# Retention plus GELU MLP on one core: w_out cast on two engines, batch 1's values cast by ScalarE, batch 2 turned by DMA

## The chip, the cores and the metric

The kernel runs on one core of a Trainium2 chip. The metric is the device time of one execution in microseconds (us); it was 302.02 us as the median of three executions (301.77 to 302.8). TensorE (PE) multiplies, VectorE (DVE), ScalarE (ACT) and GpSimd (POOL) do the elementwise work, and SyncE (SP) issues nearly all DMAs.

## The reference

For 8 batches, 8 heads, 576 positions and 64 values per head, a retention layer without a softmax feeds a two-layer MLP:

```
scores = (q @ k^T) / sqrt(64)                       # per batch and head, 576 x 576
ret    = scores * gamma[h]^(i-j) for i >= j, else 0  # gamma[h] = 1 - 2^(-5-h)
x      = (ret @ v), heads side by side               # 4608 tokens x 512
out    = gelu_tanh(x @ w_in) @ w_out                 # 512 -> 2048 -> 512
```

All inputs and the output are float32; the kernel computes in float16 with float32 sums.

## The kernel before, in words

**Blocks.** The MLP works on nine blocks of 512 tokens, t = 0 to 8. Block t < 8 is the first 512 positions of batch t; block 8 gathers the 64 last positions ("tails") of all batches. The retention of batch t + 1 is computed inside block t, in pieces that are hung between the MLP's steps. The 512 positions are four chunks of 128; a chunk's result needs its scores (`score`, `score2`, PE, tile `st`), the masked scores (`masks`, `masks2`, DVE, tile `ret`), and the running state of the chunks before it (`state`, `state2` on PE, tile `us`; `scan` on DVE, tiles `vs` and `ws`; `spread` on ACT, tile `tbd` or `tbt`). `past` and `av` / `av2` on PE add both into tile `xs`, and `put` on ACT writes `xT`, the MLP's input. `later` is `scan` and then `spread`.

**Order.** Every engine runs its instructions in the order in which the program emits them. A block is a list of steps, and `at(t, u, f)` hangs f behind step u of block t; negative u are the steps of block 0's first MLP half. Block 0: steps 0 to 15 are `down_mm` for output rows 0 to 255 (two matmuls each, one per f of w_out's 16 rows of tiles), step 16 is `store_pair`, steps 17 to 32 are `down_mm` for the other rows, step 33 is the second `store_pair`. Block 1: steps 0 to 15 are `up_half` (eight matmuls and one GELU each), then 14 steps `prod(m, u)` for the seven products of a Strassen-like scheme in the order 1, 6, 5, 7, 2, 3, 4, two halves u each. Blocks 2 to 8: steps 0 to 15 are `up`, then the same 14 steps. Products 1 and 2 sum into PSUM tile `opA`, 6, 7 and 4 into `opB`, 5 and 3 into `opC`; `after` (L574 adds on DVE, L590 and L604 copies on ACT) reads a sum out before the next product of that tile may write. `act_sums` (DVE, L542 to L545) makes the summed activations `s` that products 3, 5, 6 and 7 use, and `weight_sums` (DVE, L531) the summed weights `wt`.

**Loads.** All loads of q, k, v, w_in and w_out go through 16 buffers `ld` of 256 KB, in the order of the list `seq`: batch 0, 16 tiles of w_in, 16 of w_out, then batch by batch. A load may be issued once the buffer's former tile has been cast, and SP has at most 8 transfers in flight: each waits for the landing of the one eight before it. `pump` emits the loads that have a buffer, `q_ld["hold"]` stops it until `resume`. `cast` (line L251, L253, L256 or L264, called by `cc`) turns a loaded tile into float16 tiles `cq`, `ck`, `cv`, scaled by the decay for q and k. Batches 0 to 2 (`b < NPE`) are loaded so that two neighbouring positions come as one piece of 512 bytes; the others come in pieces of 256 bytes. `cq` has one buffer, `ck` and `cv` two.

**Turning.** Scores need q and k with the 64 values of a head on the partitions (tile `tt`). In batches 0 to 2 PE does that: `turn` is eight 128x128 transposes into a PSUM tile `tr` and one copy on ACT (L291), once for q and once for k in each half (group g) of a batch. From batch 3 on `turn_dma` has SP issue one DMA transpose for `ck` and one for `cq`, of 16 blocks of 128x128 each; in every second block a third one follows for two batches' tails (`ett`).

**Around the change.** The 16 casts of w_out (L630) are on POOL, behind four memsets (L710) and ahead of the mask constants `cm`, `tm` and all casts of batches 1 and 2. Batch 1's q is turned behind steps 19 and 32 of block 0 and k behind step 21 and step 0 of block 1; batch 2's turns hang behind steps 8, 9, 13 and 14 of block 1. Batch 3 is cast by POOL from step 16 of block 1 on, behind a one-element copy `gate` that waits for the last `act_sums`; its DMA transposes are emitted behind step 27.

Of the kernel before, what the change touches and what calls it, by code (L numbers as in the profile page):

```python
# [20 lines left out]
def kernel(  # L21
# [20 lines left out]
    W = NC * 512  # L42
    NB = W // 128
    NPE = 3
    LD = 16
    HOLD = 3
    TB = 512
    NI = TB // 128
    NTB = NT // TB
# [32 lines left out]
    def load_tails(b):  # L82
        a = att[PAIR + b] = {"raw": {}, "ret": {}}
        for key in "kqv":
            a["raw"][key, 0] = t = ldt()
            for n in range(2):
# [2 lines left out]
                    in_=SRC[key][b + n, :, M0:S, :].rearrange("h s d -> s h d"),  # L89
                )  # L90

    def load(b, key, c):
        src = SRC[key]
        t = lds()
        if b < NPE:
            g, y = c // 2, c % 2
            nc.sync.dma_start(  # L97
                out=t.rearrange("p (n x) -> p n x", n=4),
                in_=src[b, y::2, 256 * g : 256 * g + 256, :].rearrange("n (p j) d -> p n (j d)", j=2),
            )  # L100
        else:
            nc.sync.dma_start(
                out=t.rearrange("p (h d) -> p h d", d=D),
                in_=src[b, :, 128 * c : 128 * c + 128, :].rearrange("h s d -> s h d"),
            )
        att[b]["raw"][key, c] = t
# [11 lines left out]
        w_raw["o", f] = t  # L118

    def body(b):  # L120
        if b < NPE:
            return [("b", b, key, 2 * g + y) for g in range(2) for key in "qkv" for y in range(2)]
        return [("b", b, key, c) for c in range(NC) for key in "kqv"]

    seq = body(0) + [("i", g, ct) for g in range(4) for ct in range(4)]
    seq += [("o", f) for f in range(NF)]
    TP = {2: 0, 4: 2, 6: 4, 7: 6}
    for b in range(1, B):
        seq += body(b)
# [4 lines left out]
    def pump(freed=0):  # L134
        q_ld["free"] += freed
        while q_ld["next"] < len(seq) and not q_ld["hold"]:
            s = seq[q_ld["next"]]
            if s[0] != "t":
                if q_ld["free"] == 0:
                    return  # L140
                q_ld["free"] -= 1
            q_ld["next"] += 1
            {"b": load, "i": load_w_in, "o": load_w_out, "t": load_tails}[s[0]](*s[1:])
# [101 lines left out]
    def cast(b, key, c, eng):  # L245
        a = att[b]
        raw = a["raw"].pop((key, c))
        dst = a[key][:, 512 * c : 512 * c + 512]
        if key == "v":
            if eng is nc.scalar:  # L250
                eng.copy(out=dst, in_=raw)  # L251
            else:
                eng.tensor_copy(out=dst, in_=raw)  # L253
        elif b < NPE:
            y = c % 2
            eng.tensor_tensor(  # L256
                out=a[key][:, 1024 * (c // 2) : 1024 * (c // 2) + 1024].rearrange("p (n l d) -> p l n d", l=2, d=D)[:, y],
                in0=raw.rearrange("p (n d) -> p n d", d=D),
                in1=sp[key][:, :, y].unsqueeze(2).to_broadcast([128, 8, D]),
                op=ALU.mult,  # L260
            )
        else:
            s0 = {"q": 0, "k": 2}[key] + (b >= PAIR)
            eng.tensor_tensor(  # L264
                out=dst.rearrange("p (h d) -> p h d", d=D),
                in0=raw.rearrange("p (h d) -> p h d", d=D),
                in1=sc[:, s0].unsqueeze(2).to_broadcast([128, 8, D]),
                op=ALU.mult,
            )
# [21 lines left out]
            cp(out=o, in_=t)  # L291
            drop(full)

    def turn_dma(b, tails=None):
        a = att[b]
        for key in "kq":
            nc.sync.dma_start_transpose(out=a["t" + key], in_=a[key])
        if tails is not None:
            cast_tails(tails)

    def resume():
        q_ld["hold"] = False
        pump()

    def tq(b, c, p):
        return att[b]["tt"][:, 1, 8 * (c // 2) + 2 * p + c % 2 if b < NPE else 4 * c + p, :]

    TILES = [(h, hl) for h in range(2) for hl in range(2)]

# [109 lines left out]
    def spread(b, c, cp):  # L419
        w = att[b].pop(("w", c))  # L420
        for hl in range(2):
            r = slice(64 * hl, 64 * hl + 64)
            cp(out=(tbd[b % 2][r, c, :, r] if c < NC - 1 else tbt[b % NT4][r, :, r]), in_=w[r])  # L423
# [78 lines left out]
        return sb.tile([128, 2, DM], F32, tag="ost", name="ost", bufs=2)  # L502

    def down_mm(t, i, f):
        if f == 0:
            op[i] = bank("op")
        nc.tensor.matmul(op[i], gT[t][:, f, i], w_out_sb[:, f, :], start=(f == 0), stop=(f == NF - 1))  # L507

    def store_pair(t, i0, eng):
        o = ost()  # L510
# [11 lines left out]
    W11, W12 = w_out_sb[:, 0:NH, 0:HD], w_out_sb[:, 0:NH, HD:DM]  # L522
    W21, W22 = w_out_sb[:, NH:NF, 0:HD], w_out_sb[:, NH:NF, HD:DM]

    def weight_sums(f):
        s = slice(f, f + 4)
        for o, x, y, f in (
            ("1", W12, W11, ALU.subtract), ("3", W22, W12, ALU.subtract),
            ("2", wt["3"], W11, ALU.add), ("4", W21, wt["2"], ALU.subtract),
        ):  # L530
            nc.vector.tensor_tensor(out=wt[o][:, s], in0=x[:, s], in1=y[:, s], op=f)  # L531

    gs = {}
# [87 lines left out]
    def cast_w(kind, *i):  # L621
# [10 lines left out]

    WENG = {
        "i": (nc.gpsimd.tensor_copy,),
        "o": (nc.gpsimd.tensor_copy,),
    }

    def cc(b, key, c, eng):
# [63 lines left out]
    def at(t, u, f, last=False):  # L702
        events.setdefault((t, u, last), []).append(f)
# [3 lines left out]
            f()  # L707


    at(0, -12, lambda: [nc.gpsimd.memset(x, 0.0) for x in (tbd[1][:, 1:], *tbt[1:])])  # L710
    for f in range(NF):
        at(0, -5 + f // 4, lambda f=f: cast_w("o", f))


    def group(b, g, at_, own=True, ahead=()):
        (t0, q), (t1, k), (t2, s), (t3, o) = at_
        at(t0, q, lambda: turn(b, g, "q", (A.copy,)))
        at(t1, k, lambda: turn(b, g, "k", (A.copy,)))

        def first():  # L720
            if own:
                state2(b, g)
            score2(b, g)
            if own:
                later(b, 2 * g)
            masks2(b, g, 0), masks2(b, g, 1)
            if own:
                scan(b, 2 * g + 1)

        def second():  # L730
            past(b, 2 * g), past(b, 2 * g + 1), av2(b, g)
            for x in ahead:
                state2(*x)
            put(b, 2 * g), put(b, 2 * g + 1)

        at(t2, s, first)
        at(t3, o, second)
        if own:
            at(t3, o + 1, lambda: spread(b, 2 * g + 1, A.copy))
        for n, y in ahead:  # L740
            at(t3, o + 1, lambda: [later(n, 2 * y + h) for h in range(2)])

    def casts2(b, g, us):
        for (t, u), (key, y) in zip(us, [(key, y) for key in "qkv" for y in range(2)]):
            at(t, u, lambda key=key, y=y: cc(b, key, 2 * g + y, P))

    at(0, 0, chunk_masks)
    at(0, 8, lambda: (new_casts(1), new_turned(1)))
    at(0, 14, lambda: weight_sums(0))
    casts2(1, 0, [(0, x) for x in (15, 15, 16, 16, 17, 17)])  # L750
    group(1, 0, ((0, 19), (0, 21), (0, 23), (0, 31)))
    casts2(1, 1, [(0, x) for x in (27, 27, 28, 28, 29, 29)])
    group(1, 1, ((0, 32), (1, 0), (1, 1), (1, 6)))
    at(1, 2, lambda: (new_casts(2), new_turned(2)))
    casts2(2, 0, [(1, x) for x in (4, 4, 5, 5, 6, 6)])
    at(1, 8, lambda: weight_sums(4))
    group(2, 0, ((1, 8), (1, 9), (1, 12), (1, 18)), ahead=((2, 1),))
    casts2(2, 1, [(1, x) for x in (9, 9, 10, 10, 11, 11)])
    group(2, 1, ((1, 13), (1, 14), (1, 20), (1, 26)), own=False)

    at(6, 0, lambda: load_tails(TP[7]))
    at(6, 18, lambda: cast_tails(TP[7]))
# [72 lines left out]
    for t in range(NTB):  # L835
        steps = []
        if t == 0:
            for i0, f0, f1 in ((0, 0, NF), (2, 0, NF)):
                for f in range(f0, f1):
                    steps.append(lambda f=f, i0=i0: [down_mm(0, i0 + n, f) for n in range(2)] and None)  # L840
                if f1 == NF:
                    steps.append(lambda i0=i0: store_pair(0, i0, (A.copy, V.tensor_copy)))
        else:
            for u in range(2 if t == 1 else 0):
                for f in (0, NH, 2, NH + 2, 4, NH + 4, 6, NH + 6):
                    def half(u=u, f=f):
                        up_half(t, u, f)
                        if f in (NH + 2, NH + 6):
                            return lambda: act_sums(t, f - NH - 2, f - NH + 2, slice(u, u + 1))
                    steps.append(half)  # L850
            for f in range(0 if t == 1 else NH):
                steps.append(lambda f=f: up(t, f))
                def hi(f=f):
                    up(t, f + NH)
                    if f % 2:
                        return lambda: act_sums(t, f - 1, f + 1)
                steps.append(hi)
            for m in (1, 6, 5, 7, 2, 3, 4):
                for u in range(2):
                    steps.append(lambda m=m, u=u: (prod(t, m, u), after(t, m, u)))  # L860
        for u, s in enumerate(steps):
            then = s()
            run(t, u)
            if callable(then):
                then()
            run(t, u, True)
# [31 lines left out]
```

## Time and profile before

| what | value |
|---|---|
| median of 3 executions | 302.02 us |
| the profiled execution | 302.57 us, of which the span of the program 300.6 us |
| PE busy | 285.1 us (95%) |
| DVE, ACT, POOL busy | 165.8, 163.5, 107.1 us |
| DMA queue of SP | 51.92 MB, 73.4% of 16 engines' span |
| granted TensorE clock | 1.000 |

The span counts from the program's first to its last instruction; times inside it are given from its start. "Idle before" is the time an engine stood still before an instruction, and the releaser is what ended it. A DMA's issue is SP's work; it lands some microseconds later.

### The profile page before, as it was taken

The page shows a single profiled execution, that of the slowest core. Times are in us where ns is not written, and L with a number is a line of the kernel's source. Part 1 is how long each engine was busy: PE and PEld are TensorE (multiplying, and loading weights), DVE is VectorE, ACT ScalarE, POOL GpSimd, SP SyncE. Part 2 cuts the span into 40 slices and gives each one's busy share as a digit, 9 for nine tenths or more (in the row PEclk, how much of TensorE's full clock was granted, in tenths as well). Part 3 has the DMA queues.
Part 4 walks back from the last instruction along what each step waited for, and adds up shares of the span by engine and source line. Part 5 has one row for each costly group of instructions (what it writes and reads, how often), then busy time and mean ns, then how long its engine had stood idle before and what let it go on. Part 6 is the DMA issues. An engine that isn't in the chain of part 4 may idle for free.

```text
span 300.6 us, 7300 instructions
## 1 busy us (share of the span) xinstructions
PE 285.1 (95%) x3028; PEld 197.2 (66%) x3028; DVE 165.8 (55%) x339; ACT 163.5 (54%) x300; POOL 107.1 (36%) x145
## 2 busy tenths in 40 slices
PE   6789979899989999999999999999999999999993
PEld 2458635688875488548854885478547854884583
DVE  5770335698654865475548654855486635332432
ACT  5377323988627673666466746664666256306500
POOL 4689998950690065005800550058020000000000
PEclk9999999999999999999999999999999999999999
DMA  7999999998759999989899949944931030002004
GB/s 207 313 367 386 359 289 301 289 246 189 158 94 207 230 217 181 262 195 197 145 237 228 185 91 265 219 92 83 258 82 37 3 140 0 2 38 105 0 0 140
DMA packets 129056, 52.89 MB, mean 176 GB/s; under 512 B 101632, under 2 KB 120576, under 8 KB 129024
## 3 DMA queue, kind: packets, MB, share of 16 engines
q1 hardware_dynamic: 128544, 51.92, 73.4%
q10 hardware_dynamic: 480, 0.52, 0.6%
q8 instruction: 23, 0.38, 0.5%
q14 instruction: 9, 0.07, 0.1%
HBM read 36.70 MB, written 9.44 MB: 153 GB/s over the span
## 4 chain that ended last, share of the span: by engine, by line
PE 76%; POOL 6%; DMA 6%; DVE 4%; ACT 4%; SPq 3%; issue 1%; POOLq 0%; DVEq 0%; ACTq 0%
PE hp L469 29%; PE opB L560 13%; PE opC L560 9%; PE opA L560 9%; PE hp L487 4%; DMA ld<-in_moe_w_in_dram 4%; POOL w_out_sb L630 4%; SPq L97 3%; PE xs L448 2%; PE st L372 2%; DMA ld<-in_v_dram 2%; PE xs L439 2%; PE op L507 1%; ACT gT L475 1%; PE us L397 1%
## 5 line engine op out<-in xcount | busy, mean ns | idle before, releaser
L469 PE MATMUL hp<-xT,w_in_sb 128*128 128x512 f16 x448 | 99.0, 379 | 0.3 <-DVE ret L381 0.3
L475 ACT ACTIVATE gT<-hp 128x512 f16<-128x512 f32 x112 | 64.9, 597 | 46.3 <-PE hp L469 45.8
L469 PEld LDWEIGHTS <-w_in_sb 128*128 128x128 f16 x448 | 43.3, 98 | 51.1 <-issue 0.6
L560 PEld LDWEIGHTS <-gT 128*128 128x128 f16 x512 | 49.6, 98 | 6.9 <-issue 0.7
L560 PEld LDWEIGHTS <-s 128*128 128x128 f16 x384 | 36.4, 98 | 6.3 <-issue 1.2
L542 DVE TENSOR_TENSOR s<-gT 128x512 f16<-128x512 f16 x32 | 14.4, 450 | 46.4 <-ACT gT L475 44.0
L823 POOL COPY gate<-s 128x1 f16<-128x1 f16 x5 | 0.9, 188 | 94.7 <-DVE s L545 80.8
L560 PE MATMUL opB<-wt,gT 128*128 128x256 f16 x256 | 30.7, 273 | 0.5 <-DVE ost L574 0.5
L487 PE MATMUL hp<-xT,w_in_sb 128*128 128x256 f16 x256 | 30.3, 273 | 0.8 <-POOL w_in_sb L630 0.4
L560 PE MATMUL opA<-w_out_sb,gT 128*128 128x256 f16 x256 | 30.6, 273 | 0.0
L423 ACT CAST tbd<-ws 64x256 f16<-64x256 f32 x48 | 19.3, 403 | 15.0 <-DVE ws L414 14.3
L487 PEld LDWEIGHTS <-w_in_sb 128*128 128x128 f16 x256 | 24.3, 98 | 4.5 <-POOL w_in_sb L630 0.9
L381 DVE TENSOR_TENSOR ret<-st,cm 128x512 f16<-128x512 f32 x40 | 24.8, 681 | 0.0
L458 ACT CAST xT<-xs 128x512 f16<-128x512 f32 x36 | 19.3, 591 | 9.3 <-PE xs L362 7.6
L604 ACT COPY ost<-opA 128x512 f32<-128x512 f32 x8 | 4.7, 585 | 35.7 <-PE opA L560 26.2
L574 DVE TENSOR_TENSOR k<-k,opB 128x512 f32<-128x512 f32 x16 | 11.0, 687 | 21.8 <-PE opB L560 15.8
L574 DVE TENSOR_TENSOR ost<-k,opC 128x512 f32<-128x512 f32 x16 | 11.0, 687 | 21.0 <-PE opC L560 20.7
L264 POOL TENSOR_TENSOR cq<-ld,sc 128x512 f16<-128x512 f32 x20 | 21.7, 1085 | 0.0
L493 ACT ACTIVATE gT<-hp 128x512 f16<-128x512 f32 x32 | 19.1, 605 | 4.7 <-PE hp L487 4.5
L264 POOL TENSOR_TENSOR ck<-ld,sc 128x512 f16<-128x512 f32 x20 | 20.8, 1039 | 0.0
L414 DVE TENSOR_TENSOR ws<-vs,gt 128x256 f32<-128x256 f32 x24 | 15.9, 665 | 1.2
L560 PE MATMUL opC<-w_out_sb,s 128*128 128x256 f16 x128 | 15.5, 273 | 1.0 <-DVE ost L574 1.0
(92 smaller groups left out, 351.3 us busy)
## 6 DMA issues: line engine op xcount, KB each, us to landing
ld<-in_q_dram SPq DMA_DIRECT2D x32, 256.0 KB, 5.4
ld<-in_k_dram SPq DMA_DIRECT2D x32, 256.0 KB, 5.3
ld<-in_v_dram SPq DMA_DIRECT2D x32, 256.0 KB, 5.4
out_dram<-ost SPq DMA_DIRECT2D x16, 512.0 KB, 3.5
ld<-in_moe_w_in_dram SPq DMA_DIRECT2D x16, 256.0 KB, 5.7
ld<-in_moe_w_out_dram SPq DMA_DIRECT2D x16, 256.0 KB, 5.5
lt<-in_k_dram SPq DMA_DIRECT2D x8, 128.0 KB, 5.6
lt<-in_q_dram SPq DMA_DIRECT2D x8, 128.0 KB, 4.3
```

Source lines behind the costliest of these rows:

```text
L264: eng.tensor_tensor(out=dst.rearrange("p (h d) -> p h d", d=D), in0=raw.rearrange("p (h d) -> p h d", d=D), in1=sc[:, s0].unsqueeze(2).to_ ...
L381: nc.vector.tensor_tensor(out=r.rearrange("p (n i) -> p n i", i=128), in0=t.rearrange("p (n i) -> p n i", i=128), in1=(cm if b < PAIR else ...
L414: nc.vector.tensor_tensor(out=w, in0=uc, in1=gt, op=ALU.mult)
L423: cp(out=(tbd[b % 2][r, c, :, r] if c < NC - 1 else tbt[b % NT4][r, :, r]), in_=w[r])
L458: nc.scalar.copy(out=xT[:, g0 : g0 + 2], in_=xs.rearrange("p (n g t) -> p g n t", n=HP, g=2))
L469: nc.tensor.matmul(hp.rearrange("p (g t) -> p g t", t=TL), w_in_sb[:, ct, 128 * fc : 128 * fc + 128], xT[:, o : o + TB // TL, ct, :], star ...
L475: nc.scalar.activation(out=gT[t][:, fc].rearrange("p i n -> p (i n)"), in_=hp, func=AF.Gelu_apprx_tanh)
L487: nc.tensor.matmul(hp[:, 256 * x : 256 * x + 256].rearrange("p (g t) -> p g t", t=TL), w_in_sb[:, ct, 128 * (f + x) : 128 * (f + x) + 128] ...
L493: nc.scalar.activation(out=gT[t][:, f : f + 2, 2 * u : 2 * u + 2, :].rearrange("p f i n -> p f (i n)"), in_=hp.rearrange("p (f n) -> p f n ...
L542: nc.vector.tensor_tensor(out=s["1"], in0=a21, in1=a22, op=ALU.add)
L560: nc.tensor.matmul(op[tag][:, HD * u : HD * u + HD], lhs(f), rhs[:, f], start=(new and u == 0 and f == 0), stop=(f == NH - 1), skip_group_ ...
L574: nc.vector.tensor_tensor(out=o, in0=a, in1=b, op=ALU.add)
```

## The change

w_out's 16 tiles are loaded and cast in the order `FO` = 0-3, 8-11, 4-7, 12-15, alternately by POOL and DVE, and `down_mm` sums in that order; the first four weight sums are spread between DVE's casts. The memsets of `tbd[1]` and `tbt[1:]` move from POOL to DVE, the mask constants to block 1. Batch 1's v is cast by ACT, its q and k by POOL as before, and its turns, scores and outputs hang behind other steps. Batch 2's q is loaded in pieces of 256 bytes, its k and v as before; q and k are cast by POOL in a row, and two DMA transposes (q, then k) replace PE's four turns. They are emitted behind step 31 of block 0, ahead of the second `store_pair`; batch 2's v and batch 3 are held back until they are issued. In blocks 1 to 7 the last products are 2, 4, 3 instead of 2, 3, 4.

```diff
+    NTE = 2
+    def paired(b, key):
+        return b < NTE or (b < NPE and key != "q")
     def load(b, key, c):
-        if b < NPE:
+        if paired(b, key):
...
     def body(b):
+        if b < NTE:
+            return [("b", b, key, 2 * g + y) for g in range(2) for key in "qkv" for y in range(2)]
         if b < NPE:
-            return [("b", b, key, 2 * g + y) for g in range(2) for key in "qkv" for y in range(2)]
+            return [("b", b, key, c) for key in "qk" for c in range(NC)] + [("h",)] + [("b", b, "v", c) for c in range(NC)] + [("h",)]
...
-    seq += [("o", f) for f in range(NF)]
+    FO = [f + g for f in (0, 4) for g in (0, 1, 2, 3, 8, 9, 10, 11)]
+    seq += [("o", f) for f in FO]
...
+            if s[0] == "h":
+                q_ld.update(hold=True, next=q_ld["next"] + 1)
+                return
...
-        "o": (nc.gpsimd.tensor_copy,),
+        "o": (nc.gpsimd.tensor_copy, nc.vector.tensor_copy),
...
-    at(0, -12, lambda: [nc.gpsimd.memset(x, 0.0) for x in (tbd[1][:, 1:], *tbt[1:])])
-    for f in range(NF):
-        at(0, -5 + f // 4, lambda f=f: cast_w("o", f))
+    at(0, -12, lambda: [V.memset(x, 0.0) for x in (tbd[1][:, 1:], *tbt[1:])])
+    for n, f in enumerate(FO):
+        at(0, -5 + n // 4, lambda f=f: cast_w("o", f))
+        if n > 8 and n % 2:
+            at(0, -5 + n // 4, lambda n=n: weight_sums(0, [(n - 9) // 2]))
...
-    at(0, 0, chunk_masks)
-    at(0, 8, lambda: (new_casts(1), new_turned(1)))
-    at(0, 14, lambda: weight_sums(0))
-    casts2(1, 0, [(0, x) for x in (15, 15, 16, 16, 17, 17)])
-    group(1, 0, ((0, 19), (0, 21), (0, 23), (0, 31)))
-    casts2(1, 1, [(0, x) for x in (27, 27, 28, 28, 29, 29)])
-    group(1, 1, ((0, 32), (1, 0), (1, 1), (1, 6)))
-    at(1, 2, lambda: (new_casts(2), new_turned(2)))
-    casts2(2, 0, [(1, x) for x in (4, 4, 5, 5, 6, 6)])
+    at(0, 6, lambda: (new_casts(1), new_turned(1)))
+    casts2(1, 0, (0, 7), (0, 19))
+    group(1, 0, ((0, 15), (0, 18)), (0, 20), (0, 29))
+    casts2(1, 1, (0, 14), (0, 27))
+    group(1, 1, ((0, 23), (0, 26)), (0, 31), (1, 3))
+    at(0, 30, lambda: (new_casts(2), new_turned(2)))
+    at(0, 30, lambda: [cc(2, key, c, P) for key in "qk" for c in range(NC)])
+    at(0, 31, lambda: (turn_dma(2, None, "qk"), resume()))
+    at(1, 0, resume)
+    at(1, 1, lambda: [cc(2, "v", c, P) for c in range(NC)])
+    at(1, 2, chunk_masks)
     at(1, 8, lambda: weight_sums(4))
-    group(2, 0, ((1, 8), (1, 9), (1, 12), (1, 18)), ahead=((2, 1),))
-    casts2(2, 1, [(1, x) for x in (9, 9, 10, 10, 11, 11)])
-    group(2, 1, ((1, 13), (1, 14), (1, 20), (1, 26)), own=False)
+    group(2, 0, (), (1, 14), (1, 19), ahead=((2, 1),))
+    at(1, 20, lambda: later(2, 2))
+    at(1, 24, lambda: later(2, 3))
+    group(2, 1, (), (1, 20), (1, 27), own=False)
...
-            for m in (1, 6, 5, 7, 2, 3, 4):
+            for m in (1, 6, 5, 7, 2, 3, 4) if t == NTB - 1 else (1, 6, 5, 7, 2, 4, 3):
```

In `group` the pairs are now the steps of the two turns (none for batch 2), of scores and state, and of the outputs; in batch 2's second group two of the four masked scores wait for one step more. `casts2(b, g, kq, v)` casts q and k by POOL at the first step and v by ACT at the second.

More of the change, by code (lines that the diff above doesn't have):

```diff
@@ L44 @@
     NPE = 3
+    NTE = 2
     LD = 16
-    HOLD = 3
     TB = 512
@@ L253, in cast @@
                 eng.tensor_copy(out=dst, in_=raw)
-        elif b < NPE:
+        elif paired(b, key):
             y = c % 2
@@ L292, in turn, with turn_dma @@
             drop(full)
-    def turn_dma(b, tails=None):
+    def turn_dma(b, tails=None, keys="kq"):
         a = att[b]
-        for key in "kq":
+        for key in keys:
             nc.sync.dma_start_transpose(out=a["t" + key], in_=a[key])
@@ L305, in tq @@
     def tq(b, c, p):
-        return att[b]["tt"][:, 1, 8 * (c // 2) + 2 * p + c % 2 if b < NPE else 4 * c + p, :]
+        return att[b]["tt"][:, 1, 8 * (c // 2) + 2 * p + c % 2 if b < NTE else 4 * c + p, :]
     TILES = [(h, hl) for h in range(2) for hl in range(2)]
@@ L504, in down_mm @@
     def down_mm(t, i, f):
-        if f == 0:
+        if f == FO[0]:
             op[i] = bank("op")
-        nc.tensor.matmul(op[i], gT[t][:, f, i], w_out_sb[:, f, :], start=(f == 0), stop=(f == NF - 1))
+        nc.tensor.matmul(op[i], gT[t][:, f, i], w_out_sb[:, f, :], start=(f == FO[0]), stop=(f == FO[-1]))
     def store_pair(t, i0, eng):
@@ L523, with weight_sums @@
     W21, W22 = w_out_sb[:, NH:NF, 0:HD], w_out_sb[:, NH:NF, HD:DM]
-    def weight_sums(f):
+    def weight_sums(f, ns=range(4)):
         s = slice(f, f + 4)
[L527 to L530, printed above, removed]
+        for n in ns:
+            o, x, y, f = (
+                ("1", W12, W11, ALU.subtract), ("3", W22, W12, ALU.subtract),
+                ("2", wt["3"], W11, ALU.add), ("4", W21, wt["2"], ALU.subtract),
+            )[n]
             nc.vector.tensor_tensor(out=wt[o][:, s], in0=x[:, s], in1=y[:, s], op=f)
@@ L707, in run, with group @@
             f()
-    at(0, -12, lambda: [nc.gpsimd.memset(x, 0.0) for x in (tbd[1][:, 1:], *tbt[1:])])
-    for f in range(NF):
-        at(0, -5 + f // 4, lambda f=f: cast_w("o", f))
[L715 to L718, printed above, removed]
+    at(0, -12, lambda: [V.memset(x, 0.0) for x in (tbd[1][:, 1:], *tbt[1:])])
[3 more added lines that the diff above has]
+            at(0, -5 + n // 4, lambda n=n: weight_sums(0, [(n - 9) // 2]))
+    def group(b, g, turns, s, o, own=True, ahead=()):
+        for w, key in zip(turns, "qk"):
+            at(*w, lambda key=key: turn(b, g, key, (A.copy,)))
         def first():
@@ L725, in first @@
                 later(b, 2 * g)
-            masks2(b, g, 0), masks2(b, g, 1)
+            masks2(b, g, 0)
             if own:
+                masks2(b, g, 1)
                 scan(b, 2 * g + 1)
+            else:
+                at(s[0], s[1] + 1, lambda: masks2(b, g, 1))
         def second():
@@ L734, in second, with casts2 @@
             put(b, 2 * g), put(b, 2 * g + 1)
-        at(t2, s, first)
-        at(t3, o, second)
+        at(*s, first)
+        at(*o, second)
         if own:
[L739 to L745, printed above, removed]
-    at(0, 0, chunk_masks)
-    at(0, 8, lambda: (new_casts(1), new_turned(1)))
-    at(0, 14, lambda: weight_sums(0))
-    casts2(1, 0, [(0, x) for x in (15, 15, 16, 16, 17, 17)])
-    group(1, 0, ((0, 19), (0, 21), (0, 23), (0, 31)))
-    casts2(1, 1, [(0, x) for x in (27, 27, 28, 28, 29, 29)])
-    group(1, 1, ((0, 32), (1, 0), (1, 1), (1, 6)))
-    at(1, 2, lambda: (new_casts(2), new_turned(2)))
-    casts2(2, 0, [(1, x) for x in (4, 4, 5, 5, 6, 6)])
+            at(o[0], o[1] + 1, lambda: spread(b, 2 * g + 1, A.copy))
+    def casts2(b, g, kq, v):
+        at(*kq, lambda: [cc(b, key, 2 * g + y, P) for key in "qk" for y in range(2)])
+        at(*v, lambda: [cc(b, "v", 2 * g + y, A) for y in range(2)])
+    at(0, 6, lambda: (new_casts(1), new_turned(1)))
[9 more added lines that the diff above has]
+    at(1, 2, chunk_masks)
     at(1, 8, lambda: weight_sums(4))
-    group(2, 0, ((1, 8), (1, 9), (1, 12), (1, 18)), ahead=((2, 1),))
-    casts2(2, 1, [(1, x) for x in (9, 9, 10, 10, 11, 11)])
-    group(2, 1, ((1, 13), (1, 14), (1, 20), (1, 26)), own=False)
+    group(2, 0, (), (1, 14), (1, 19), ahead=((2, 1),))
+    at(1, 20, lambda: later(2, 2))
+    at(1, 24, lambda: later(2, 3))
+    group(2, 1, (), (1, 20), (1, 27), own=False)
     at(6, 0, lambda: load_tails(TP[7]))
@@ L837 @@
         if t == 0:
-            for i0, f0, f1 in ((0, 0, NF), (2, 0, NF)):
-                for f in range(f0, f1):
+            for i0 in (0, 2):
+                for f in FO:
                     steps.append(lambda f=f, i0=i0: [down_mm(0, i0 + n, f) for n in range(2)] and None)
-                if f1 == NF:
-                    steps.append(lambda i0=i0: store_pair(0, i0, (A.copy, V.tensor_copy)))
+                steps.append(lambda i0=i0: store_pair(0, i0, (A.copy, V.tensor_copy)))
         else:
```

## The prediction

> **What bounds the kernel now.** I read the page's busy shares first. PE has work 95% of the span at a granted clock of 1.000, so a gain must come out of PE's 15.5 us of idle time or out of work taken from it. The view of waits says where PE stood still; these four lines are the ones that the change can reach:
>
> ```profile
> PE tr L285 <- POOL cq L256: 1.9, 2, 1.3
> PE st L321 <- ACT tt L291: 1.5, 2, 1.3
> PE opC L560 <- DVE ost L574: 1.0, 1, 1.0
> PE tr L285 <- POOL ck L256: 0.5, 1, 0.5
> ```
>
> The columns are total us, times, longest us. PE's timeline places them:
>
> ```profile
> 43.09 0.62 PE L285 MATMUL tr<-ident,cq 128*128 128x128 f16 x8 [1.26 <-POOL cq L256]
> 45.10 0.62 PE L285 MATMUL tr<-ident,ck 128*128 128x128 f16 x8 [0.53 <-POOL ck L256]
> 57.01 0.64 PE L321 MATMUL st<-tt 64*64 64x128 f16 x32 [1.29 <-ACT tt L291]
> 85.94 1.03 PE L560 MATMUL opC<-w_out_sb,s 128*128 128x256 f16 x8 [1.04 <-DVE ost L574]
> ```
>
> All lie between 33.3 us (block 0's `down_mm`) and 91 us (end of block 1). Two waits of 0.18 us for xT make it 4.3 us. The rest of PE's idle time is the start, up to 20 us, and the last stores, where the order of work stays as it is. So block 0's second half and block 1 are the stage to read. Next, POOL's timeline there: it casts w_out without a pause and goes from the last of them straight to batch 1:
>
> ```profile
> 26.68 0.95 POOL L710 MEMSET tbd<- 128x1024 f16 x1
> 27.57 1.46 POOL L710 MEMSET tbt<- 128x512 f16 x3
> 28.97 10.80 POOL L630 CAST w_out_sb<-ld 128x512 f16<-128x512 f32 x16
> 40.98 2.05 POOL L256 TENSOR_TENSOR cq<-ld,sc 128x512 f16<-128x512 f32 x2
> ```
>
> Last, the DMAs by stretches (the last three columns: granted clock, busy share of the 16 engines, GB/s), and SP's queue at the end of block 1:
>
> ```profile
> 65.00:70.00 5.00, 5.00 (x92) 4.43 (x93) 4.08 (x9) 4.96 (x9) 0.00 (x0) 1.00 1.00 209
> 85.00:90.00 5.00, 4.06 (x80) 3.55 (x80) 1.47 (x3) 1.64 (x3) 5.00 (x7) 1.00 0.23 37
> ```
>
> ```profile
> 90.13 0.38 SPq L577 DMA_DIRECT2D out_dram<-ost  x1
> 90.62 3.30 SPq L297 DMA_TRANSPOSE tt<-ck  x1
> 94.02 1.82 SPq L297 DMA_TRANSPOSE tt<-cq  x1
> 95.93 1.86 SPq L241 DMA_TRANSPOSE ett<-e  x1
> ```
>
> The DMAs are full from the start to about 75 us; they idle around 87 us, where SP waits with a store for DVE. Batch 3's three transposes land at 95.95, 98.39 and 99.61 us by the trace's landing records, and PE takes them up at 99.65 (`tt`) and 100.11 us (`ett`). That is a second path to the same place, with 0.5 us to spare.
>
> **The change on PE's path.** Four turns of batch 2 go: 4 x 0.45 us of eight transposes each = 1.8 us, and their four ACT copies with them. The waits:
>
> Batch 1's q, 1.26 us. w_out's last tile landed at 37.13; with half the casts on DVE, POOL is through about 1 us after it instead of at 39.8. Batch 1's first four tiles landed at 38.10, 38.88, 39.78 and 40.69; four casts of 1.05 us from 38.3 on end at 39.4, 40.4, 41.5, 42.5. The turn of q now comes at step 15, at 33.3 + 32 x 0.2225 = 40.5 us: no wait, 0.3 at most. That DVE's casts hold POOL up is in this: w_out casts beside DVE's weight sums took 1.07 us instead of 0.61, and four such make 1.8 us at most, which would end q at 41.5 and cost 1 us. I take 0.
>
> Batch 1's k, 0.53 us. PE is at step 18 at 40.5 + 0.45 + 0.9 = 41.85, k is cast at 42.5: 0.6 us remain.
>
> A new wait: batch 1's v on ACT. `state2` comes behind step 20, at 42.5 + 0.45 + 0.9 = 43.9. ACT has queued ahead of the casts of v the copy of turned q, the copy of block 0's output (0.58) and the copy of turned k; turned k was copied 1.67 us after its first transpose, so at 44.2, and two casts at 0.61 end at 45.4. PE waits 1.4 us (0 if ACT's copies were early, 1.7 at most). Behind it in ACT's queue stands only `spread`.
>
> Batch 1's second half: q and k landed by 44.3 and 46.0, are cast by 45.5 and 47.6, and are turned at 47.7 and 49.5, so the 1.29 us for ACT's copy of `tt` go, and the 0.36 for xT. In their place `score2` waits for PSUM: its last two banks are those of `xs`, which ACT empties behind two casts of v (about 0.3 us), and block 1's second `up_half` takes the bank of the first masked score (about 0.2 us). Bounds for both: 0 and 0.9.
>
> Batch 2. Its scores come at step 14 of block 1, near 70 us, and the turned q and k land by 63 (below). But product 6 now follows product 1 with nothing between, while DVE must first mask batch 2's scores (4 x 0.62) and scan them (0.85) and then add twice (0.42 each) to make `s` for the second half. From `state2` at 69.5 that is 73.8 to 76 us, by whether `weight_sums` and the adds run beside POOL (1.27 us for an add that takes 0.42 alone); PE wants it at 73.9. I take 1.4 us, bounds 0 and 2.2.
>
> Product 4 in front of 3: DVE reads `opB` out before `opC`, so the 1.04 us go and nothing comes in place; in blocks 2 to 7 PE waited for neither before. The chunk masks on POOL at step 2 of block 1, the memsets on DVE at 21 us, where DVE idles until 31, and ost's reuse have cover of several us: nothing.
>
> Sum for PE: -1.8 - 1.26 + (0.6 - 0.53) + 1.4 - 1.29 - 0.36 + 0.5 + 1.4 - 1.04 = -2.4 us. With all new waits at their upper ends it is +0.1, with all at 0 it is -6.3.
>
> **The change on the DMAs' path.** Batch 1's last tile lands at 47.8 in both kernels (0.88 us per tile, as before). From there, tile by tile: batch 2's q, now in pieces of 256 bytes, 4 x 1.17 = 4.7 (1.17 from batch 4's first four tiles, 81.93 to 86.61); k 4 x 0.88 = 3.5; a store 1.4; the two transposes 2.4 each (95.95 to 98.39), 4.8. SP meets a wait here that was not there: the transposes stand behind POOL's casts, q's done near 53.7 and k's at 58, and v of batch 2, the second store and all of batch 3 stand behind them. Issued at 58, k's transpose lands 4.4 to 5.3 us later, at 62.4 to 63.3, where the sum alone gives 62.2: 0.6 us lost. Then v 3.5; a store 1.5; batch 3's 12 x 1.17 = 14.0; six half-size tail tiles 3.6; batch 4's first four 4.7; block 1's store 1.4; batch 3's transposes 2.5 + 2.4 + 1.2 = 6.1. In all 47.8 + 49.8 = 97.6 us for `ett`, against 99.61 before and with no idle stretch left. PE, 2.4 us earlier, asks for it at 100.1 - 2.4 = 97.7. The two paths meet, and the forecast is their meeting with 0.2 us for the two not missing each other: **-2.2 us**. From block 2 on all engines shift together; batch 4's casts begin 2 us earlier and its last tile lands 2 us earlier, too.
>
> The Trainium skill, VectorE: DVE Perf Modes, section "The three transpose paths", gives 1309 ns for a DMA transpose of 128x128 and 390 ns for TensorE's. By that figure, an estimate, 16 blocks in a row would take 20.9 us, k's would land near 95 us, and block 1 would stand still for some 25 us. The trace's 2.4 us per 16 blocks decides against it.
>
> Profiled execution: 302.57 - 2.2 = 300.4 us; it stood 0.55 over the median of 302.02, so the time is **299.8 us**.
>
> **Rivals.** A change of up to 0.3% (0.9 us) counts as none.
>
> A, the new waits don't come: DVE and ACT keep up, PE gains 3.3 to 5, and the DMAs are quicker too (1.07 us per tile saves 2). For it: a wait on ACT needs three queued instructions to meet. 297.2 to 298.7 us. Chance 0.20.
>
> B, nothing left over: the waits at `state2`, product 6 and the PSUM banks sit near their upper ends and eat 1.8 us of transposes. 301.1 to 302.9. Chance 0.18.
>
> C, slower: batch 3's transposes come late. Between 59.93 and 86.61 before, 16 tiles of 256-byte pieces took (26.7 - 1.5 - 3.7) / 16 = 1.34 us each, partly because SP waited for buffers. If 1.34 is the DMAs' own price, 20 tiles cost 3.4 us more, `ett` lands at 101.0, and PE's scores of batch 3 wait until then: +0.9 us, 302.9, and 304 if SP's issue of a transpose takes 3.3 us twice. It decides from 1.29 us per tile on. Against it: SP's waits for those buffers are gone by then. Chance 0.16.
>
> The forecast with 298.7 to 301.1 has 0.46.
>
> **How the numbers follow.** Faster by over 0.9: forecast and A, 0.66. Same 0.18, slower 0.16. Leaving out the lower half of A and the upper part of C, the range is 297.6 to 303.0.
>
> **What would show it.** PE's transposes x64 and not x96; two more DMA transposes of `tt`, issued near 54 and 58; no wait of opC for ost in block 1; a wait of PE for ACT's cast `cv` near 44, and one of opB for `s` near 74; the DMA share near 1 through 90 us, and scores of batch 3 taken up within a microsecond of `ett`'s landing, at 97 to 98. If `ett` lands 3 us before PE asks, the DMA sum is wrong; if the first wait for `cq` is still over 1 us, the casts are.

## The result, and the profile after

The changed kernel took 306.32 us (median of four, 305.21 to 307.49) against 302.01 before: 1.0138 times the time, interval 1.0095 to 1.0182, 4.3 us slower where 2.2 us less was forecast. Its profiled execution took 306.71 us with a span of 305.0, 4.4 us over the span before, at a mean granted clock of 0.993. One execution each of e4, e5 and e10 below ran in a slower state of the chip (e5's was the profiled one, at a granted clock of 0.562), and their medians and ratios are those of the other executions.

First the view of waits, PE's rows (total us, times, longest us):

```profile
PE st L381 <- DMA tt<-cq: 4.2, 1, 4.2
...
PE tr L294 <- POOL cq L265: 1.8, 2, 1.3
...
PE us L357 <- ACT cv L260: 1.2, 2, 0.9
PE opB L570 <- DVE s L553: 1.0, 1, 1.0
...
PE tr L294 <- POOL ck L265: 0.5, 1, 0.5
...
PE st L381 <- DMA ett<-e: 0.4, 1, 0.4
```

The waits for ACT's copy of `tt` (1.29 us) and of opC for `ost` (1.04) are gone, the two new waits that were forecast are there (`cv`, `s`), and ahead of them all stands one that was put among the rivals: the scores of batch 3 wait for a DMA transpose. PE's timeline shows where it stands:

```profile
42.48 0.62 PE L294 MATMUL tr<-ident,cq 128*128 128x128 f16 x8 [1.34 <-POOL cq L265]
...
46.86 0.18 PE L357 MATMUL us<-cv,ck 64*64 64x64 f16 x1 [0.88 <-ACT cv L260]
...
76.83 0.61 PE L570 MATMUL opB<-wt,s 128*128 128x256 f16 x4 [1.02 <-DVE s L553]
...
89.47 8.80 PE L478 MATMUL hp<-xT,w_in_sb 128*128 128x512 f16 x40
102.47 0.67 PE L381 MATMUL st<-tt 64*128 64x128 f16 x16 [4.20 <-DMA tt<-cq]
103.58 0.61 PE L381 MATMUL st<-ett 64*128 64x128 f16 x8 [0.44 <-DMA ett<-e]
104.12 6.42 PE L478 MATMUL hp<-xT,w_in_sb 128*128 128x512 f16 x24
```

The same stretch of the kernel before:

```profile
90.92 8.80 PE L469 MATMUL hp<-xT,w_in_sb 128*128 128x512 f16 x40
99.65 0.62 PE L372 MATMUL st<-tt 64*128 64x128 f16 x16
100.11 0.39 PE L372 MATMUL st<-ett 64*128 64x128 f16 x8
100.43 5.35 PE L469 MATMUL hp<-xT,w_in_sb 128*128 128x512 f16 x24
```

Block 2 begins at 89.47, where it began at 90.92 before: up to here the change had won 1.45 us. The next 24 up-projections began at 100.43 before and begin at 104.12 now, and they take 6.42 us instead of 5.35. So 1.45 us won, 5.14 lost at the wait (the waits are 4.64 of it), 1.07 lost in matmuls that are slower than before: 4.8 us, of which 4.4 are seen at the end. The slower matmuls show in the windows of 1 us (after the five engines' busy times: granted clock, DMA share, GB/s):

```profile
101.00:102.00 1.00, 0.00 (x0) 0.00 (x0) 0.00 (x0) 0.00 (x0) 0.00 (x0) 1.00 1.12 213
...
103.00:104.00 1.00, 0.56 (x12) 0.34 (x8) 1.00 (x2) 0.00 (x0) 0.00 (x0) 0.50 1.01 342
104.00:105.00 1.00, 1.00 (x7) 0.33 (x4) 1.00 (x3) 0.00 (x0) 0.00 (x0) 0.50 0.94 187
...
106.00:107.00 1.00, 1.00 (x6) 0.41 (x4) 0.56 (x1) 0.60 (x1) 0.00 (x0) 0.84 1.31 249
```

After 4 us of standing still PE was granted half its clock for about 3 us. Why the transposes were late is on SP's queue and on DVE:

```profile
88.16 0.57 SPq L105 DMA_DIRECT2D ld<-in_k_dram  x1
88.83 1.28 SPq L105 DMA_DIRECT2D ld<-in_q_dram  x1
90.21 1.22 SPq L105 DMA_DIRECT2D ld<-in_v_dram  x1
91.52 1.26 SPq L105 DMA_DIRECT2D ld<-in_k_dram  x1
92.86 1.03 SPq L587 DMA_DIRECT2D out_dram<-ost  x1
94.00 3.87 SPq L306 DMA_TRANSPOSE tt<-ck  x1
97.97 1.93 SPq L306 DMA_TRANSPOSE tt<-cq  x1
99.98 1.73 SPq L250 DMA_TRANSPOSE ett<-e  x1
```

```profile
86.81 0.69 DVE L584 TENSOR_TENSOR ost<-k,opB 128x512 f32<-128x512 f32 x1 [1.51 <-PE opB L570]
```

DVE had the block's first output ready at 87.50. SP issued its store at 92.86, 5.4 us later: four loads of batch 4 stood ahead of it in order, and three of them took 1.2 to 1.3 us each to issue, at a DMA share of 1.07 from 88 to 93 us. Before, SP idled there and issued the store at 90.13, as soon as DVE was through at 90.07:

```profile
89.38 0.69 DVE L574 TENSOR_TENSOR ost<-k,opC 128x512 f32<-128x512 f32 x1 [3.50 <-PE opC L560]
```

From the store to `ett`'s landing it is 10.7 us now (92.86 to 103.54) and was 9.5 (90.13 to 99.61): the transposes themselves cost little more, they began late.

### The profile page after: what moved, and what is told of

Same layout as the page of the kernel before. It is cut to its first block, busy times and chain, and to the rows that moved or that the text cites. A ratio compares the mean times of both kernels' runs of the same rounds, so it can differ in the third digit from the quotient of the medians.

```text
span 305.0 us, 7225 instructions
## 1 busy us (share of the span) xinstructions
PE 284.8 (93%) x2996; PEld 195.5 (64%) x2996; DVE 167.1 (55%) x351; ACT 162.0 (53%) x300; POOL 98.4 (32%) x129
## 4 chain that ended last, share of the span: by engine, by line
PE 75%; DMA 11%; DVE 5%; POOL 3%; SPq 3%; ACT 1%; issue 1%; POOLq 0%; DVEq 0%
PE hp L478 31%; PE opB L570 14%; PE opC L570 9%; PE opA L570 9%; DMA ld<-in_moe_w_out_dram 4%; DMA ld<-in_q_dram 4%; DMA ld<-in_moe_w_in_dram 2%; PE xs L457 2%; PE hp L496 2%; PE st L381 2%; SPq L306 2%; PE op L516 2%; PE xs L448 2%; POOL cq L265 1%; DMA ett<-e 1%; DVE wt L541 1%
## 5 line engine op out<-in xcount | busy, mean ns | idle before, releaser
L496 PE MATMUL hp<-xT,w_in_sb 128*128 128x256 f16 x256 | 29.5, 273 | 1.6 <-POOL w_in_sb L640 1.3
L273 POOL TENSOR_TENSOR cq<-ld,sc 128x512 f16<-128x512 f32 x24 | 25.8, 1079 | 1.6 <-DMA ld<-in_q_dram 1.6
L570 PE MATMUL opB<-wt,s 128*128 128x256 f16 x128 | 15.5, 273 | 1.0 <-DVE s L553 1.0
L423 DVE TENSOR_TENSOR ws<-vs,gt 128x256 f32<-128x256 f32 x24 | 15.0, 624 | 1.2
```

Of the source, the lines that this page charges most:

```text
L273: eng.tensor_tensor(out=dst.rearrange("p (h d) -> p h d", d=D), in0=raw.rearrange("p (h d) -> p h d", d=D), in1=sc[:, s0].unsqueeze(2).to_ ...
L423: nc.vector.tensor_tensor(out=w, in0=uc, in1=gt, op=ALU.mult)
L496: nc.tensor.matmul(hp[:, 256 * x : 256 * x + 256].rearrange("p (g t) -> p g t", t=TL), w_in_sb[:, ct, 128 * (f + x) : 128 * (f + x) + 128] ...
L570: nc.tensor.matmul(op[tag][:, HD * u : HD * u + HD], lhs(f), rhs[:, f], start=(new and u == 0 and f == 0), stop=(f == NH - 1), skip_group_ ...
```

## The experiments

The theory: the change's gain on PE is real, and all of it and more is lost at one place, where block 1's store and batch 3's transposes stand behind batch 4's first loads on SP's queue. The rival: the loss is spread (slower engines, the new waits), and the late transposes only show it. The table holds the landing records and PE's waits of the profiled executions, and the medians with their ratios. The kernel before ran beside each kernel on the same chip (its medians were 302.01 to 303.03), and the ratio is to that; medians of different rows can come from different chips:

| kernel | store issued | `ett` landed | PE's waits for tt, ett | profiled us | median us | ratio [interval] |
|---|---|---|---|---|---|---|
| before | 90.13 | 99.61 | 0 | 302.57 | 302.01 | 1 |
| changed | 92.86 | 103.54 | 4.20, 0.44 | 306.71 | 306.32 | 1.0138 [1.0095, 1.0182] |
| a1_again | 91.74 | 102.69 | 5.23, 0 | 305.96 | 306.00 | 1.0118 [1.0078, 1.0158] |
| e1_b4_late | 87.71 | 98.22 | 0 | 300.64 | 299.59 | 0.9905 [0.9874, 0.9936] |
| e2_scores_late | 91.85 | 102.74 | 0.62, 0.51 | 300.87 | 300.58 | 0.9926 [0.9905, 0.9947] |
| e3_pe_turn | 87.85 | 97.25 | 0 | 300.99 | 300.32 | 0.9916 [0.9888, 0.9945] |
| e4_filler | 90.79 | 101.91 | 0 (filled), 0.49 | 303.77 | 304.74 | 1.0067 [1.0043, 1.0092] |
| e11_hold_before | 90.64 | 100.18 | 0 | 303.14 | 302.94 | 0.9998 [0.9979, 1.0016] |
| e8_cv | 88.40 | 99.00 | 2.67, 0.48 | 300.85 | 298.88 | 0.9876 [0.9841, 0.9911] |
| e10_all | 86.43 | 96.19 | 0.86, 0.45 | 298.18 | 298.18 | 0.9878 [0.9838, 0.9919] |
| e12_late2 | 86.26 | 96.27 | 0 | 296.89 | 297.01 | 0.9802 [0.9780, 0.9824] |

**a1_again: the changed kernel once more.** No edit.

> The changed kernel itself once more, for a second trace of it. In its first profiled execution batch 1's last tile landed at 50.04 us, 2.2 us later than before, and the transposes missed PE by 4.2 + 0.44 us; in eight other profiled executions of kernels with the same first loads w_out's last tile landed anywhere from 37.3 to 39.8 us. If the early loads' pace is a matter of the single execution, batch 1's last tile may land near 48 us here, ett near 101.5 to 102 instead of 103.54, and the wait is 2 to 3 us, but the median stays at 304.5 to 307. If the change makes them late, it lands at 50 again, ett at 103.5 and the wait is 4 us or more. Either way the ratio is 1.007 to 1.018.

Batch 1's last tile landed at 48.16 us this time, against 47.83 before and 50.04 in the first trace, and PE was 3.3 us ahead of before at block 2 (87.59). It helped nothing:

```profile
101.61 1.03 PE L381 MATMUL st<-tt 64*128 64x128 f16 x16 [5.23 <-DMA tt<-cq]
```

`ett` came 0.85 us earlier than in the first trace, not 1.5 to 2, and the wait was longer, because PE was there earlier: half of the expectation failed, and the ratio held. The pace of the first loads differs between executions of one kernel; the wait is there in both.

**e1_b4_late: batch 4's loads behind the transposes.**

```
         if b - 1 in TP:
             seq.append(("t", TP[b - 1]))
+        if b == NPE:
+            seq.append(("h",))
```

> Batch 4's first four loads are held until block 1's transposes are issued; all else as in the changed kernel. Theory Q (the loss is PE's wait for batch 3's transposes, which stand behind too many transfers on SP's queue): these four took 4.0 us of landings (92.25 to 96.22) ahead of the transposes, so the tails' transpose lands near 99.5 instead of 103.54, PE's wait falls from 4.6 to about 1 us, the clock stays at 1.00, and the time is near 301.5. Rival W (the waits and slower starts of block 0 and of the casts are the loss, and the transposes only show it): the time stays above 305.

SP's queue now goes from the tails straight to the store:

```profile
87.71 0.57 SPq L589 DMA_DIRECT2D out_dram<-ost  x1
88.40 4.14 SPq L308 DMA_TRANSPOSE tt<-ck  x1
92.64 1.77 SPq L308 DMA_TRANSPOSE tt<-cq  x1
94.50 1.86 SPq L252 DMA_TRANSPOSE ett<-e  x1
```

The store leaves 5.2 us earlier, `ett` lands 5.3 us earlier, PE waits for neither, and the kernel is 6.7 us quicker than the changed one by the medians. That is more than was expected: 4.6 us of waiting and 1.1 us of half clock are gone, and batch 4's loads, issued 9 us later, are not missed. The other 1.0 us is not accounted for; executions of the changed kernel alone differ by 2.3 us.

**e2_scores_late: the scores of block 2 five steps later, what follows them two to four.** No transfer is moved.

```
-        s0, o0, s1, o1 = 9, 15, 19, 25
+        s0, o0, s1, o1 = (14, 19, 23, 27) if t == 2 else (9, 15, 19, 25)
```

> In block 2 alone, batch 3's scores move from step 9 to 14 and what follows them by 2 to 4 steps; no transfer is moved. Q: PE does 4.3 us of other work while the transposes land, 0.5 us of the wait is left, the clock stays at 1.00: near 301. W: 305 to 306, as nothing of block 0 and 1 changes.

The transposes are as late as ever (102.74), but PE has 60 up-projections instead of 40 before it asks, and waits 1.13 us instead of 4.64: 5.7 us quicker than the changed kernel. That the time returns with the DMAs' lateness left as it is speaks against a spread loss.

**e3_pe_turn: batch 2 turned on PE again.**

```
-    NTE = 2
+    NTE = 3
-    at(0, 31, lambda: (turn_dma(2, None, "qk"), resume()))
-    at(1, 0, resume)
-    group(2, 0, (), (1, 14), (1, 19), ahead=((2, 1),))
+    group(2, 0, ((1, 8), (1, 9)), (1, 14), (1, 19), ahead=((2, 1),))
-    group(2, 1, (), (1, 20), (1, 27), own=False)
+    group(2, 1, ((1, 12), (1, 13)), (1, 20), (1, 27), own=False)
```

> Batch 2 is loaded in 512-byte pieces and turned by PE again (four turns, 1.8 us of PE work); everything else as in the changed kernel. Q: SP's queue is rid of two transposes (some 8 us from the last load of k to the landing of the second) and of the wait for the casts ahead of them, batch 3's transposes land some 7 us earlier, PE does not wait for them: PE is 1.45 us ahead of the kernel before at the end of block 1 and pays 1.8 us of turns, so 302 to 302.8. W: 305 or more.

Better than expected. Without batch 2's DMA transposes the tails landed at 82.83 instead of 92.25, the store left as DVE finished, and `ett` landed at 97.25. PE's 1.8 us of transposes are back, and block 2 still begins at 89.81, 1.1 us ahead of the kernel before: the change's other parts carry this gain. Turning batch 2 by DMA (its q in smaller pieces, the transposes, and what they held up behind them) had cost 9.4 us on the way to the tails, of which some 1.4 us (71.13 to 72.50 in the first trace) are block 0's second store, which goes behind the tails here. For that PE got little: e1, which keeps the DMA turns and had equally late first loads, reaches block 2 at 89.32, only 0.5 us earlier, because it waits 1.41 us for `s` ahead of product 6, where this kernel does not wait. The intervals of e1 and e3 overlap, so no run shows that the DMA turns gain anything by themselves.

**e4_filler: 14 matmuls of nothing in PE's wait.** They keep PE at work and change nothing that is computed.

```
+        if t == 2 and c == 0:
+            filler(14)
```

> 14 matmuls of 512 columns without use (3.1 us at full clock) ahead of batch 3's scores, inside the 4.2 us that PE waits there. If the halved clock after the wait is a cost of the idle time itself, it stays at 1.00, and the time falls by 1.3 us to about 305. If the clock falls for another reason, the time stays at 306.3 or rises.

```profile
97.56 3.19 PE L235 MATMUL fill<-tbd,ident 128*128 128x512 f16 x14
```

The clock stayed at 1.00 in every window from 97 to 107 us, and the 24 up-projections after the scores took 5.35 us again. The medians fell by 1.6 us (306.32 to 304.74; 306.00 in a1), where the slower matmuls had cost 1.07 us. The ratio's interval ends at 1.0092, and those of the changed kernel begin at 1.0095 and 1.0078, so the size rests on the traces.

**e11_hold_before: the hold of e1 in the kernel before.**

> A control: the kernel before, with batch 4's first loads held back as in e1_b4_late and nothing else. If e1's lead over the kernel before is the change's own gain, uncovered by the hold, the hold alone is worth nothing here: in the kernel before these four tiles landed at 86.61 us, ahead of the store, and PE did not wait for the transposes. Ratio 0.999 to 1.001, or up to 1.003 if batch 4's loads then come late. Rival: the hold alone is a gain, because the transposes go out over a free queue, ratio 0.99 to 0.997; then e1 shows nothing of the change.

Ratio 0.9998. The hold is worth nothing where the queue is not full, so e1's 0.95% is the change's own gain, uncovered.

**e5_order: before, with only the products' order changed** to 1, 6, 5, 7, 2, 4, 3.

> The kernel before with nothing but the last products swapped: 1, 6, 5, 7, 2, 4, 3 in blocks 1 to 7. In the kernel before, PE waited 1.04 us for ost ahead of opC at 85.94 us; the batch-3 transposes follow block 1's last store on SP's queue and landed 0.5 us before PE asked. If the prediction's term (-1.04 us, nothing in its place) holds: the wait is gone, store and transposes come 1 us earlier with it, time 0.9 to 1.1 us less, ratio 0.9965 to 0.997. Rival: the transposes keep their time, PE gains the 0.5 us of spare only, ratio 0.9983; or the block's end moves from PE to SP and nothing is left, 1.000.

302.04 us, ratio 0.9975 [0.9955, 0.9995]: 0.76 us less, between the term of the sum (1.04) and its rival (0.5), and the interval holds both. Only times are read from it.

**e7_wcast: before, with only w_out's casts shared** by GpSimd and VectorE.

```
-        "o": (nc.gpsimd.tensor_copy,),
+        "o": (nc.gpsimd.tensor_copy, nc.vector.tensor_copy),
```

> The kernel before with nothing but w_out's casts dealt in turn to GpSimd and VectorE. If the prediction's reading of the first waits is right, POOL is free about 2 us earlier for batch 1, and PE's waits for cq (1.26 us) and ck (0.53 us) go: 1.2 to 1.8 us less, ratio 0.994 to 0.996. Rival: w_out's last tiles land when they land and DVE's casts only stand in the way of its weight sums, so that PE waits as before: 0.999 to 1.001; in the changed kernel the wait for cq was still 1.34 us, at an earlier step of block 0.

301.06 us, ratio 0.9952 [0.9928, 0.9976], in the middle of what was expected. Its profiled execution, 304.47 us, was the longest of its ten and had a late w_out (the last tile but one landed at 39.79 us), and it still waited 0.46 us for `cq` and 0.97 for `ck`; the two add up to 0.36 less than before. The mask constants still stand on POOL ahead of batch 1's casts here (40.40 to 41.95 us). The gain is shown by the times, its mechanism not by this trace.

**e8_cv: e1 with batch 1's first values cast by DVE.**

```
-        at(*v, lambda: [cc(b, "v", 2 * g + y, A) for y in range(2)])
+        at(*v, lambda: [cc(b, "v", 2 * g + y, V if g == 0 else A) for y in range(2)])
```

> The kernel that holds batch 4's loads back (e1_b4_late), with the values of batch 1's first half cast by DVE instead of ACT. Prices of e1's profile: state2 waited 0.88 + 0.33 us for ACT's cv; DVE is idle for 4 of 5 us there. If that wait is worth its length: 1.0 to 1.2 us under e1's ratio of 0.9905, 0.9865 to 0.987. Rival: the next thing that ACT empties (the turned k, the PSUM banks of xs) takes its place, and the ratio stays at 0.99.

The wait for `cv` is gone, and the ratio moved from 0.9905 to 0.9876, by 0.9 us, but the intervals overlap. In its profile PE reached block 2 at 86.47, 2.85 us earlier than in e1 (1.2 us of it can be the first loads, with w_out's last tile at 38.02 against 39.23), and the transposes came 0.8 us later than in e1:

```profile
97.94 0.62 PE L383 MATMUL st<-tt 64*128 64x128 f16 x16 [2.67 <-DMA tt<-cq]
```

The rival's place was wrong (ACT), but a wait did take over: the same one as before.

**e10_all: e8 with batch 2's scores and outputs behind block 1's last up-projection.**

```
-    group(2, 0, (), (1, 14), (1, 19), ahead=((2, 1),))
-    at(1, 20, lambda: later(2, 2))
+    group(2, 0, (), (1, 17), (1, 21), ahead=((2, 1),))
+    at(1, 22, lambda: later(2, 2))
     at(1, 24, lambda: later(2, 3))
-    group(2, 1, (), (1, 20), (1, 27), own=False)
+    group(2, 1, (), (1, 22), (1, 28), own=False)
```

> e8_cv with batch 2's scores and outputs of both halves moved behind the last up-projection of block 1 (steps 17, 21, 22, 28 for 14, 19, 20, 27), so that DVE adds up s for product 6 before it masks and scans. In e1 PE waited 1.41 us for that s. If that wait is worth its length: 1.0 to 1.4 us less than e8_cv, ratio 0.982 to 0.9835. Rival: DVE's masks and scans come late for the outputs instead, or block 1's end is set by SP's transposes of batch 3 and nothing is gained over e8_cv.

The ratios show no gain over e8 (0.9878 and 0.9876). The wait that it was to remove had been 1.41 us in e1, but only 0.33 in e8, and it is gone here; what stays is 0.86 + 0.45 us for the transposes.

**e12_late2: e10 with the scores of block 2 two steps later, the next two steps one.**

```
-        s0, o0, s1, o1 = 9, 15, 19, 25
+        s0, o0, s1, o1 = (11, 16, 20, 25) if t == 2 else (9, 15, 19, 25)
```

> e10_all with the scores of block 2 taken two steps later (11, 16, 20 and 25 for 9, 15, 19 and 25), 1.75 us of matmuls. In e10 PE still waited 0.86 us for tt and 0.45 us for ett, in e8 2.67 and 0.48 us, in runs whose transposes were issued at 87.1 and 89.1 us. If these waits are worth their length: 1.0 to 1.3 us less than e10, ratio 0.983 to 0.984, with no wait for tt. Rival: the steps behind it move together and something later in block 2 waits (outputs, the casts of batch 4), and the ratio stays at 0.988.

297.01 us, ratio 0.9802, better than expected; all four runs lie within 0.4 us. Under e10 it is 1.2 us by the medians and 2.3 by the ratios, where the waits had been 0.86 + 0.45 us. PE goes from the up-projections to the scores with no wait:

```profile
85.54 10.52 PE L480 MATMUL hp<-xT,w_in_sb 128*128 128x512 f16 x48 [0.18 <-ACT xT L469]
```

This version beats both kernels: the one before by 2.0% (1.8 to 2.2), and the changed one by 3.3% if the two ratios to the kernel before are divided.

## Why the prediction was wrong

**The step that failed is the sum on the DMAs' path**, which put `ett`'s landing at 97.6 us; it landed at 103.54 and 102.69. Its terms, predicted and then measured in the two traces of the changed kernel:

| term | predicted | first trace | second trace |
|---|---|---|---|
| batch 1's last landing | 47.8 | 50.04 | 48.16 |
| from there to batch 2's k turned (q, k, store, two transposes, gap) | 15.0 | 16.7 | 17.5 |
| v and the second store | 5.0 | 5.8 | 5.6 |
| batch 3, 12 tiles | 14.0 | 14.95 | 14.94 |
| six tail tiles | 3.6 | 4.8 | 4.95 |
| batch 4's four tiles | 4.7 | 3.97 | 3.91 |
| store, three transposes | 7.5 | 7.3 | 7.7 |

The largest error in both traces together is the way to batch 2's turned k, 1.7 and 2.5 us over. The text had k's transpose issued at 58 us; it was issued at 61.01 and 60.20, behind a transpose of q that held SP for 5.4 and 5.7 us and k's casts that ended at 59.74 and 60.09, and its own issue then kept batch 2's v back until 64.07 and 63.51. Batch 1's last landing adds 2.2 us in the first trace and 0.4 in the second. The rest is small: 1.245 us per tile of batch 3 stands against 1.17, and the tails took a third more. Five of the seven errors in the first trace and six in the second have one sign; all seven add up to 5.9 and 5.1 us. By the prediction's terms the tails land at 85.4 us, 3.5 us later than before; they landed at 92.25 and 91.11, and at 82.83 in e3, without the DMA turns. Each price was that of a good stretch of the trace before, and the sum was laid against PE's 97.7 us with 0.2 us for missing it. The range admitted an error of 3.4 us on this path, through rival C alone. The text saw that nothing would be idle any more, and it counted batch 4's loads ahead of the store; it did not ask what else of that queue could wait. Batch 4's four tiles were 4 us of the path, and e1 shows that they had no need to be there.

**The second error is what a miss costs.** Rival C charged the miss at its length. The runs show 1.07 us on top for the clock. The Trainium skill, TensorE: Matmul & The Clock Gate, section "What's actually happening", states that the clock falls to half after an idle window of about 3.4 us and needs about as much work to return. The rows agree in part: a gap of 4.20 us here and of 5.23 us in a1 brought the granted clock to 0.50, and in e8 a gap of 2.67 us left it at 1.00. But the length of one gap does not decide alone. In a1 the clock fell within the window from 98 to 99 us, less than 3 us after PE had stopped at 96.4; in the first trace it fell near the end of the window from 102 to 103 (0.95), after PE had started again; and in e3 it stood at half for about 3.4 us after 20.5 us, where no gap of PE just before was longer than 0.55 us. Windows of a1, e8 and e3, in this order:

```profile
98.00:99.00 1.00, 0.00 (x0) 0.00 (x0) 0.00 (x0) 0.00 (x0) 0.00 (x0) 0.80 0.75 143
97.00:98.00 1.00, 0.07 (x3) 0.10 (x5) 0.00 (x0) 0.00 (x0) 0.00 (x0) 1.00 1.13 220
20.00:25.00 5.00, 5.00 (x63) 3.90 (x62) 1.78 (x6) 2.90 (x6) 4.56 (x8) 0.66 0.97 264
```

Neither the prediction nor its rivals considered the rule.

**Rival C** named the right place and sign and put 302.9 to 304 us on it, with a point of decision of 1.29 us per tile. Batch 3's tiles stayed below that point, and the wait came all the same, from the other terms of the sum.

**PE's path was right.** Forecast as 2.4 us gained by the end of block 1, it was 1.45 in the first trace and 3.3 in the second, around the forecast. Point by point: turns x64 as said; the wait at `state2` for ACT's values 0.88 + 0.34 us (1.4 said); product 6 for `s` 1.02 and 1.16 (1.4 said); `ck` 0.53 (0.6 said); the waits for `tt` and `ost` gone; no more than 0.29 us behind the masks (0.5 for the banks said). `cq` was to be free and cost 1.34 us in the first trace, where the tiles had landed 2 us late; it does not appear at that step in the second. DVE's casts took 0.43 us each and its sums 0.68; POOL's casts beside the sums took 0.78 to 0.80 us instead of 0.61, so DVE held POOL up by 0.2 us each, far less than the 1.07 us that bounded it. The times of e5 and e7 carry the same message: these two parts alone give 0.25% and 0.48%. Two readings in the text were off without moving the sum: the waits listed at its start add up to 4.5 us, not 4.3, and POOL did not go straight from w_out to batch 1 but set the mask constants between 39.72 and 41.0 us, which the change moved away as well.

## What to carry to other kernels

When a change fills the last idle stretch of a queue, what stands in order behind the new work becomes a path of its own. Sum it with pessimistic prices, because the errors of many small terms on a full queue had nearly all one sign here, and ask of every transfer ahead of the critical one whether it must be there: moving four loads behind three transposes turned 1.4% lost into 1.0% gained. Price a stall of PE by the stall and by the slower matmuls after it, and give a consumer that is next to a late transfer some other work first.

## What had not been expected of the hardware

A pair of DMA transposes of 16 blocks each holds up SP's queue by its issue: batch 3's pair for 5.0 to 6.2 us in the traces of this case (3.3 to 4.3 for the first, 1.7 to 2.0 for the second), and batch 2's, which is issued while the loads before it still land, for 7.1 to 9.0 us (4.3 to 5.9 and 2.6 to 3.4). Yet the second of a pair lands only 1.6 to 3.5 us after the first. Batch 2's v, next in order, was issued in the first trace at 64.07 us, 5.6 us after the last tile of k had landed (58.42). Why the first of these pairs takes longer to issue was not tried; in later pairs of the kernel before it is the second that does (1.4 to 1.9 and 2.4 to 4.2 us).

The pace of the very first loads differs between executions of kernels that issue the same loads: w_out's last tile landed between 37.13 and 39.26 us in eleven traces of this case, two of them of the changed kernel (39.24 and 37.33), and still later in e7. Single executions of a kernel differ by up to 3 us; whether these loads are the reason no run shows, and why they differ was not tried.
